# Attention value products in 64 by 64 tiles, with a newly planned order, in a fused attention and Hyena kernel on one core

## The chip, the cores and the metric

The kernel runs on one core of one Trainium2 chip. The metric is the device time in microseconds (us) of one execution; the median of three executions of the kernel before is 388.55 us (387.85 to 391.75). Smaller is better. All figures below come from these runs or from one execution that the hardware profiler recorded.

## The reference

Eight batches, twelve heads, 448 positions, head width 64. Attention with a softmax whose denominator has one more term, then a gated long convolution along the positions, with one projection in front and one behind:

```python
scores = scale * np.matmul(q, k.transpose(0, 1, 3, 2))      # (8, 12, 448, 448)
m = np.max(scores, axis=-1, keepdims=True)
e = np.exp(scores - m)
attn = e / (np.sum(e, axis=-1, keepdims=True) + np.exp(-m) + 1e-09)
x = np.matmul(attn, v)                                      # heads side by side: (8, 448, 768)
proj = x @ w_proj                                           # (8, 448, 2304)
x1, x2, x3 = ...                                            # three parts of 768 columns
x2_conv = irfft(rfft(x2) * rfft(filter_fft))                # along the 448 positions
out = (x1 * x2_conv * x3) @ w_out                           # (8, 448, 768) float32
```

Multiplied through by exp(m), the denominator is the plain sum of exp(scores) plus 1; this is how the kernel computes it, without a maximum.

## The kernel before

**Heads and groups.** The twelve heads of a batch form six pairs (`hp`, or `i` counted over all batches, 48 in all) and three groups of four heads (`Q`, 24 in all), each group two pairs (`u` = 0, 1). The 448 positions are split as 7 residues `j` of 64 positions each, because position p is row p // 7 and residue p % 7 of the tile as it is loaded (`load_rows`). Two heads of a pair sit in the lower and the upper 64 partitions (`w` = 0, 1).

**One group.** q, k and v of the group are loaded (L359) and cast to bf16 (L365, L370). q and k are transposed into `kqT`: on TensorE for the first two batches (L410, copied back at L415), by a transposing DMA afterwards (L426). Then come seven score units (`scores`, L597): in each, four matmuls of 64 by 64 weights and 448 moving columns stand abreast in the four quadrants of the array and write a pair of PSUM banks, and ScalarE takes the exponential of the pair into one of eleven `e` tiles (`exps`, L601). When all seven are there, each pair's value product follows (`values`, L616): 4 blocks of 128 positions, 7 residues and 2 heads make 56 matmuls. Each has 64 by 128 weights (a slice of `e`) and 65 moving columns (64 of v and one of ones, which gives the sum), and the two heads run abreast in the two row halves. The fourth block has only 64 positions, and its other 64 weight columns are zeros or the next head's: `e` is 64 columns longer than needed (`pads`, L1082). The result of a pair lies in a pair of banks, (128 positions, head, block, 65).

**Division and transposition.** VectorE adds one to the sums (L672), takes the reciprocal (L673) and multiplies (L674), pair by pair, into `xb`. `xb` is transposed into `xT`: in batch 0 on TensorE (L703, back at L712), in batches 1 to 7 by a DMA for three pairs at a time (L694).

**The dense part** of a batch (`dense`) folds `xT` on VectorE (L756, L761), projects it (`proj2`, L784), takes the spectrum (L811), multiplies (L825, L831), transforms back (`inverse`, L896), unfolds (L914 to L925), gates with the other two projections (`gate`, L857) and projects out (`project`, L969).

**The order.** No queue order is written down by hand. Every piece of work is a task with an engine, an estimated cost, a wanted time, tokens that it needs and makes, and PSUM banks that it takes and gives back; `Plan.run` is a list scheduler that goes through estimated time and fixes the order on each engine. Constants such as `ATT`, `SLOT`, `DENSE`, `PACE` and `LEAD` give the wanted times, `LOADS` and `LOAD` those of the weight loads. Eight PSUM banks are shared: a score unit and a value product take a pair (`sc`, `op`, two at most of each), all else one bank (`hy`). From the 22nd score unit on, scores come in runs of two units, and 42 of the 48 value products are "hosted": emitted in the same task right behind a run of scores (`score_runs`). While inputs are awaited at the start, `spin` (L1064 to L1073) and `fill` (L1055) issue idle matmuls. In `spin` some of them have 64 by 64 weights and 65 columns, some 64 by 128 weights and 65 columns.

The profile's names: PE is TensorE's matmul, PEld its weight load; each matmul of this kernel has a weight load of its own in front of it.

Of the kernel before, what the change touches and what calls it, by code (L numbers as in the profile page):

```python
# [256 lines left out]
def kernel(  # L257
# [15 lines left out]
    SPIN = 38  # L273
    EARLY0 = -7.81
    EARLY1 = -31.53
    NSINGLE, HOST = 22, 3
    ATT = [61.68, 19.06, 51.44, 90.48, 134.71, 184.75, 265.58, 265.83]
    SLOT = [7.18, 10.43, 5.20, 5.03, 0.93, 2.35, 4.65, 2.49]
    DENSE = [32.35, 109.75, 123.73, 146.53, 223.55, 274.11, 331.19, 326.09]
    PACE = [3.95, 1.73, 2.46, 3.56, 2.92, 2.20, 0.96, 1.78]  # L280
    FOLD = [-33.07, 7.97, -54.75, 19.23, -27.96, -50.67, -61.51, -23.76]
    BPS = -9.13
    WT = 12.35
    FT = -42.18
    LEAD = [25.24, 37.06, -25.73, 55.99, 16.70, 47.21, -33.20]
    VLATE = -3.09
    LOADS = ((1, 0), (1, 1), ("F", None), (0, None), (2, None), ("O", None))
    LOAD = [19.70, 3.41, 13.35, 32.51, 35.06, 49.84]
    XALL = (1, 2, 3, 4, 5, 6, 7)
    FOLD0 = [47.70, 1.87, 54.60]  # L290
# [6 lines left out]
    xbp = ctx.enter_context(tc.tile_pool(name="xbp", bufs=2))  # L297
# [26 lines left out]
    es = [const.tile([128, 2 * S + REM], BF16, name=f"e{i}") for i in range(NE)]  # L324
    rooms = [const.tile([128, 7 * 128], F32, name=f"room{i}") for i in range(NROOM)]
    kqn = [const.tile([128, 2, 7 * 128], BF16, name=f"kqn{i}") for i in range(NNAT)]
# [3 lines left out]
            "e": NE, "kqn": NNAT, "u": 1, "w": 1, "xf": 1,  # L330
# [43 lines left out]
    def arrive(b, g):  # L374
# [5 lines left out]
        for m, (name, x) in enumerate((("k", k), ("q", q), ("v", v))):  # L380
            n = 3 * Q + m
            to = rooms[n % NROOM]
            first = Q == 0 and name == "q"
            lead = LEAD[2 * m : 2 * m + 2] if not staged else (
                (EARLY0 if b == 0 else EARLY1) - 0.1 * m - (VLATE if m == 2 and b == 0 else 0),
                (-1.0 if b == 0 else 4.0) if m == 2 else 5.0,
            )
            add("ACT" if first else "SP", 0.6 if first else 0.52, -21.0 if Q == 0 and m < 2 else at - lead[0],
                lambda x=x, to=to, first=first: load_rows(nc.scalar if first else nc.sync, x, b, g, to),
                need=[("c" + "kqv"[(n - NROOM) % 3], (n - NROOM) // 3)] if n >= NROOM else [],  # L390
                make=[("s" + name, Q)], dma=1.35, run=1792)
            if name == "v":
                add("POOL", 0.96, at - lead[1], lambda to=to: cast_values(b, g, to), need=[("sv", Q)] + old,
                    make=[("cv", Q)])
                continue
            eng = "DVE" if Q == 0 else "POOL"

            def cast(m=m, to=to, eng=eng):
                cast_rows(nc.vector if eng == "DVE" else nc.gpsimd, kqn[Q % NNAT][:, m], to)

            add(eng, 0.56 if eng == "DVE" else 0.96, at - lead[1] + 0.01 * m, cast, need=[("s" + name, Q)], make=[("c" + name, Q)],
                take=[("kqn", Q)])
            if staged:
                hy = ("hy", ("T" + name, Q))

                def turn(m=m, hy=hy):
                    tb = bank2(hy)
                    for j in range(7):
                        c = slice(128 * j, 128 * j + 128)
                        nc.tensor.transpose(tb[:, c], kqn[Q % NNAT][:, m, c], ident_bf)  # L410

                on_act = False

                def turned(m=m, hy=hy, on_act=on_act):
                    (nc.scalar.copy if on_act else nc.vector.tensor_copy)(  # L415
                        kqT[b % 2][:, g, m].rearrange("p j c -> p (j c)"), bank2(hy)[:, 0 : 7 * 128]
                    )

                w = at - (3.5 if Q else 6.0)
                add("PE", 0.45, w, turn, need=[("c" + name, Q), "ident"], make=[("T" + name, Q)], take=[hy],  # L420
                    give=[("kqn", Q)])
                add("ACT" if on_act else "DVE", 0.83 if on_act else 0.55, w + 0.1, turned, need=[("T" + name, Q)],
                    make=[("kqT", Q)], give=[hy])
        if not staged:
            add("SP", 2.0, at - LEAD[6],
# [4 lines left out]
                need=[("ck", Q), ("cq", Q), ("S", Q - 2 * NQ, 6)], make=[("kqT", Q)], give=[("kqn", Q)], dma=1.7, late=0.5)  # L430
# [168 lines left out]
    def exps(n):  # L599
        EX[n] = e = es[n % NE]  # L600
        nc.scalar.activation(  # L601
            e[:, 0 : 2 * S].rearrange("p (u n j) -> p u n j", u=2, j=7),
# [4 lines left out]

    def values(i):
        Q, u = divmod(i, 2)
        b, g = divmod(Q, NQ)  # L610
        op = pair(("op", i))[:, :, 0 : NST * (DH + 1)].rearrange("p w (n d) -> p w n d", n=NST)
        for n in range(NST):
            for j in range(7):
                for w in range(2):
                    c = slice(64 * w, 64 * w + 64)
                    nc.tensor.matmul(  # L616
                        op[:, w, n, :],
                        EX[7 * Q + j][c, u * S + n * 128 : u * S + n * 128 + 128],
                        vn[b % 2][c, 2 * g + u, j, :],
                        start=(n == 0 and j == 0),  # L620
                        stop=(n == NST - 1 and j == 6),
                    )

    def value_args(i):
        Q, u = divmod(i, 2)
        return dict(
            need=[("e", Q), ("cv", Q), ("ones", Q // NQ % 2), "pads"] + ([("V", i - 1)] if u else []), make=[("V", i)],
            take=[("op", i)], give=[("e", 7 * Q + j) for j in range(7)],
        )

    def score_runs():
# [8 lines left out]
        for r, ns in enumerate(runs):  # L640
# [10 lines left out]
            add("PE", 0.2 + 0.155 * len(ns) + (1.0 if i is not None else 0.0), tau(2 * units[0][0], units[0][1] * 2 / 7), run,  # L651
# [6 lines left out]
        for i in range(2 * NQ * n_batches):  # L658
            if i not in hosted.values():
                a = value_args(i)  # L660
                add("PE", 1.1, tau(i // 2 * 2 + 2, 0.1 + 0.3 * (i % 2)), lambda i=i: values(i), need=a["need"], make=a["make"], take=a["take"],
                    give=a["give"])

    def attention(i):
        b, hp = divmod(i, NHP)

        def norm():
            op = pair(("op", i))[:, :, 0 : NST * (DH + 1)].rearrange("p w (n d) -> p w n d", n=NST)
            if ("xb", b) not in W:
                W["xb", b] = xbp.tile([128, NHP, NST, 128], BF16, name="xb")  # L670
            rec = small.tile([128, 2, NST], F32, name="rec")
            nc.vector.tensor_scalar_add(rec, op[:, :, :, DH], 1.0)  # L672
            nc.vector.reciprocal(rec, rec)  # L673
            nc.vector.tensor_tensor(  # L674
                W["xb", b][:, hp].rearrange("p n (w d) -> p w n d", w=2),
                op[:, :, :, 0:DH],
                rec[:].unsqueeze(3).to_broadcast([128, 2, NST, DH]),
                op=ALU.mult,
            )

        w = tau(i + 2, 0.5)
        add("DVE", 1.03, w - 0.5, norm,
            need=[("V", i)] + ([("X", NHP * (b - 1) - 1)] if b >= 2 else []),
            make=[("xb", i)], give=[("op", i)])
# [6 lines left out]
        def x_dma():  # L691
            x, xb = xT(), W["xb", b]
            gs = slice(hp - 2, hp + 1)
# [6 lines left out]
        def x_pe():  # L700
            tb = bank2(("hy", ("X", i)))
            for t in range(NST):
                nc.tensor.transpose(  # L703
                    tb[:, t * 128 : (t + 1) * 128], W["xb", b][:, hp, t, :], ident_bf
# [12 lines left out]
        if b in XALL:  # L717
            if hp % 3 == 2:
                ps = range(hp - 2, hp + 1)
# [8 lines left out]
    def dense(b):  # L728
# [213 lines left out]
        def I(dt):  # L942
# [3 lines left out]
            add("PE", 0.2, w, lambda: inverse(dt, hy), need=[("yh", b), "bt"], make=[("I", b, dt)], take=[hy],  # L946
# [89 lines left out]
    with (  # L1036
# [15 lines left out]

        def fill(i, count):
            for _ in range(count):
                nc.tensor.matmul(psum[:, 512 * i : 512 * i + 128], idle[:, 0:128], idle[:, 0:128])  # L1055
# [3 lines left out]
        def spin():  # L1059

            t = pair(("op", "spin"))
            half = (slice(0, 64), slice(64, 128))
            for _ in range(SPIN // 2):
                nc.tensor.matmul(t[:, 0, 0:128], idle, idle)  # L1064
            for _ in range(SPIN // 4):
                for u, r in enumerate(half):
                    for c in half:
                        nc.tensor.matmul(t[c, u, 0:65], idle[r, c], idle[r, 0:65])
            for _ in range(SPIN // 4):
                for u, r in enumerate(half):  # L1070
                    nc.tensor.matmul(t[:, u, 0:65], idle[r], idle[r, 0:65])
            for _ in range(SPIN // 4):
                nc.tensor.matmul(t[:, 0, 0:128], idle, idle)  # L1073

        add("PE", 4.0, -20.0, spin, need=["idle"], make=["spin"], take=[("op", "spin")], give=[("op", "spin")])
# [4 lines left out]
        def pads():  # L1080
            for e in es:
                nc.gpsimd.memset(e[:, 2 * S :], 0.0)  # L1082

        add("POOL", 1.5, 7.0, pads, make=["pads"], after=6.5)

        def ones(i):
            nc.gpsimd.memset(vn[i][:, :, :, DH : DH + 1], 1.0)
        for i in range(2):
            add("POOL", 0.7, (6.0, 24.0)[i], lambda i=i: ones(i), make=[("ones", i)],
# [52 lines left out]
```

## Time and profile before

| | |
|---|---|
| median of three executions | 388.55 us (387.85 to 391.75) |
| profiled execution: time / span | 387.59 us / 385.8 us |
| busy: PE, PEld | 370.8 us (96%), 228.2 us (59%) |
| busy: DVE, ACT, POOL | 257.8 us (67%), 258.9 us (67%), 75.9 us (20%) |
| instructions: PE matmuls, DVE, ACT | 5197, 658, 429 |
| DMA | 64.0 MB, mean 166 GB/s |
| mean granted TensorE clock | 0.991 |

The span runs from the first to the last instruction; 1.8 us of the time lie around it. A group of the profile is a line, an engine and an operation with its shapes: `64*128 64x65` are 64 by 128 weights, 64 rows of contraction and 65 moving columns. "xN | busy, mean | idle" are the count, the time in which at least one of the group was running, the mean duration of one, and the engine's idle time just before them with what ended it. Matmuls overlap in the pipeline, so 2688 value matmuls with a mean of 191 ns are busy for 51.5 us only. "issue" as releaser means that nothing the profile shows was waited for.

### The profile page before, as it was taken

The page shows a single profiled execution, that of the slowest core. Times are in us where ns is not written, and L with a number is a line of the kernel's source. Part 1 is how long each engine was busy: PE and PEld are TensorE (multiplying, and loading weights), DVE is VectorE, ACT ScalarE, POOL GpSimd, SP SyncE. Part 2 cuts the span into 40 slices and gives each one's busy share as a digit, 9 for nine tenths or more (in the row PEclk, how much of TensorE's full clock was granted, in tenths as well). Part 3 has the DMA queues.
Part 4 walks back from the last instruction along what each step waited for, and adds up shares of the span by engine and source line. Part 5 has one row for each costly group of instructions (what it writes and reads, how often), then busy time and mean ns, then how long its engine had stood idle before and what let it go on. Part 6 is the DMA issues. An engine that isn't in the chain of part 4 may idle for free.

```text
span 385.8 us, 12193 instructions
## 1 busy us (share of the span) xinstructions
PE 370.8 (96%) x5197; PEld 228.2 (59%) x5197; DVE 257.8 (67%) x658; ACT 258.9 (67%) x429; POOL 75.9 (20%) x100
## 2 busy tenths in 40 slices
PE   8969999979999999999999999999999999999996
PEld 6645675546645566556755566555755566657553
DVE  6677568884599539775689456784587355895760
ACT  4847858857687676767768667766768757644543
POOL 6746323132323321303201220010000000000000
PEclk9996999999999999999999999999999999999999
DMA  8999999999999998879556825412011302311024
GB/s 257 319 281 316 267 265 218 223 235 321 249 256 282 282 327 188 196 148 247 144 149 174 175 95 134 87 42 83 3 42 43 124 3 63 62 42 42 2 82 163
DMA packets 82998, 64.00 MB, mean 166 GB/s; under 512 B 56637, under 2 KB 79360, under 8 KB 82944
## 3 DMA queue, kind: packets, MB, share of 16 engines
q1 hardware_dynamic: 78192, 57.35, 57.3%
q0 software_dynamic: 4480, 5.41, 8.0%
q8 instruction: 40, 0.66, 0.7%
q10 hardware_dynamic: 272, 0.46, 0.3%
q14 instruction: 14, 0.11, 0.1%
HBM read 43.86 MB, written 11.01 MB: 142 GB/s over the span
## 4 chain that ended last, share of the span: by engine, by line
PE 79%; DVE 14%; ACT 2%; issue 2%; DMA 1%; DVEq 0%; ACTq 0%
PE psum L857 24%; PE psum L784 15%; PE psum L969 13%; PE psum L616 10%; PE psum L597 9%; PE psum L811 2%; PE psum L896 2%; ACT e L601 2%; DVE t L825 2%; DVE xb L674 2%; DVE cv L925 1%; PE psum L410 1%; DMA room<-in_k_dram 1%; DVE g L872 1%; DVE cw L916 1%
## 5 line engine op out<-in xcount | busy, mean ns | idle before, releaser
L601 ACT ACTIVATE e<-psum 128x896 bf16<-128x896 f32 x168 | 145.9, 922 | 33.6 <-PE psum L597 32.3
L857 PE MATMUL psum<-xT,wproj_bf 128*128 128x448 bf16 x576 | 121.7, 352 | 0.6 <-DVE xb L674 0.6
L857 PEld LDWEIGHTS <-wproj_bf 128*128 128x128 bf16 x576 | 53.0, 97 | 45.4 <-issue 3.9
L784 PE MATMUL psum<-wproj_bf,xf 128*113 128x384 bf16 x384 | 69.5, 328 | 0.0
L365 POOL CAST kqn<-room 128x896 bf16<-128x896 f32 x46 | 43.6, 950 | 105.3 <-DMA kqT<-kqn 51.4
L784 PEld LDWEIGHTS <-xf 128*113 128x113 bf16 x384 | 48.9, 132 | 14.4 <-issue 2.9
L616 PEld LDWEIGHTS <-e 64*128 64x128 bf16 x2688 | 45.4, 94 | 19.8 <-issue 18.5
L616 PE MATMUL psum<-vn,e 64*128 64x65 bf16 x2688 | 51.5, 191 | 3.1 <-issue 2.6
L969 PE MATMUL psum<-wout_bf,yT 128*128 128x384 bf16 x288 | 51.5, 326 | 2.5 <-DVE yT L940 2.5
L597 PE MATMUL psum<-kqT 64*64 64x448 bf16 x672 | 50.7, 368 | 1.3 <-DVE xb L674 0.9
L869 ACT CAST x<-psum 128x448 bf16<-128x448 f32 x48 | 25.7, 535 | 32.5 <-PE psum L857 31.5
L969 PEld LDWEIGHTS <-yT 128*128 128x128 bf16 x288 | 27.1, 98 | 23.3 <-DVE yT L940 3.7
L825 DVE TENSOR_TENSOR t<-xs,hrs 113x768 bf16<-113x768 bf16 (+1 forms) x64 | 35.6, 595 | 6.4 <-ACT xs L819 6.3
L981 ACT COPY osb<-psum 128x384 f32<-128x384 f32 x56 | 25.6, 490 | 19.7 <-PE psum L969 19.0
L796 DVE CAST x<-psum 113x384 bf16<-113x384 f32 x32 | 17.7, 554 | 30.9 <-PE psum L784 30.8
L370 POOL CAST vn<-room 128x896 bf16<-128x896 f32 x24 | 23.4, 974 | 72.3 <-PE psum L616 54.6
L872 DVE TENSOR_TENSOR g<-x,psum 128x448 bf16<-128x448 bf16 x48 | 29.6, 617 | 8.0 <-PE psum L857 7.2
L674 DVE TENSOR_TENSOR xb<-psum,rec 128x512 bf16<-128x512 f32 x48 | 33.2, 691 | 1.7
L672 DVE TENSOR_SCALAR rec<-psum 128x8 f32<-128x8 f32 x48 | 7.8, 162 | 38.2 <-PE psum L616 34.5
L819 ACT CAST xs<-psum 113x384 bf16<-113x384 f32 (+1 forms) x64 | 28.1, 500 | 4.0 <-PE psum L811 3.9
L905 ACT CAST cr<-psum 128x452 bf16<-128x452 f32 x48 | 24.8, 550 | 7.9 <-PE psum L896 6.2
L798 ACT CAST x<-psum 113x384 bf16<-113x384 f32 x32 | 15.4, 480 | 22.0 <-PE psum L784 21.8
(85 smaller groups left out, 296.9 us busy)
## 6 DMA issues: line engine op xcount, KB each, us to landing
room<-in_k_dram SPq DMA_DIRECT2D x24, 448.0 KB, 6.2
room<-in_v_dram SPq DMA_DIRECT2D x24, 448.0 KB, 5.9
room<-in_q_dram SPq DMA_DIRECT2D x23, 448.0 KB, 5.5
out_dram<-osb SPq DMA_DIRECT2D x24, 384.0 KB, 3.7
wproj_bf<-in_moe_w_proj_dram POOLq DMA_DIRECT2D x2, 1152.0 KB, 17.3
out_dram<-osb SPq DMA_DIRECT2D x8, 192.0 KB, 3.0
wproj_bf<-in_moe_w_proj_dram POOLq DMA_DIRECT2D x2, 576.0 KB, 12.9
wout_bf<-in_moe_w_out_dram POOLq DMA_DIRECT2D x1, 1152.0 KB, 17.2
```

Source lines behind the costliest of these rows:

```text
L365: eng.tensor_copy(to.rearrange("p (j u d) -> p u j d", u=2, j=7), src.rearrange("p (u j d) -> p u j d", u=2, j=7))
L597: nc.tensor.matmul(sc[c, u, 0:S], kqT[b % 2][r, g, 0, j, c], kqT[b % 2][r, g, 1, :, c])
L601: nc.scalar.activation(e[:, 0 : 2 * S].rearrange("p (u n j) -> p u n j", u=2, j=7), pair(("sc", ("S",) + divmod(n, 7)))[:, :, 0:S].rearran ...
L616: nc.tensor.matmul(op[:, w, n, :], EX[7 * Q + j][c, u * S + n * 128 : u * S + n * 128 + 128], vn[b % 2][c, 2 * g + u, j, :], start=(n == 0 ...
L674: nc.vector.tensor_tensor(W["xb", b][:, hp].rearrange("p n (w d) -> p w n d", w=2), op[:, :, :, 0:DH], rec[:].unsqueeze(3).to_broadcast([1 ...
L784: nc.tensor.matmul(pps[:FQ, :DCH], W["xf", b][:, pg, kt, 0:FQ], wproj_bf[:, kt, D + ch * DCH : D + (ch + 1) * DCH], start=(kt == 0), stop= ...
L819: nc.scalar.copy(L["xs", par, ch][:K, pg % 2, :], L["Z", pg, ch][:K, :DCH])
L825: nc.vector.tensor_tensor(t[:K], L["xs", par, ch][:K], h, op=ALU.mult)
L857: nc.tensor.matmul(p[:, :S], wproj_bf[:, kt, 2 * part * D + dt * 128 : 2 * part * D + (dt + 1) * 128], xT()[:, kt, 0:S], start=(kt == 0), ...
L869: nc.scalar.copy(L["x1", dt], p[:, :S])
L872: nc.vector.tensor_tensor(g[:, dt, :], L["x1", dt], p[:, :S], op=ALU.mult)
L969: nc.tensor.matmul(ops[:n, :DCH], y[:, dt, 0:n], wout_bf[:, dt, ch * DCH : (ch + 1) * DCH], start=(dt == 0), stop=(dt == NDT - 1),)
```

## The change

The value product of a pair is cut into blocks of 64 positions. Two such blocks are computed side by side in the two column halves of the array, so that four matmuls of 64 by 64 weights stand abreast instead of two of 64 by 128. The last 64 positions of both pairs of a group are put together as one block, so a group has 7 blocks: three in the first pair's task (84 matmuls), four in the second's (112). All results of a group lie in one pair of banks, which is taken by the first task and given back after one division for the whole group: two small operations over 2 by 7 sums and four multiplications. `e` loses its padding. The upper 64 partitions of the fourth block of `xb`, no longer written, are set to zero once; `xb` is two fixed tiles now. Transposing DMAs of `xT` cover four pairs and two pairs instead of three and three. `spin` and `fill` issue matmuls of up to 512 columns. All constants of the plan are new, and some costs in it are.

```diff
-    SPIN = 38
+    SPIN = 10
...
-    ATT = [61.68, 19.06, 51.44, 90.48, 134.71, 184.75, 265.58, 265.83]
+    ATT = [74.76, 12.23, 20.06, 84.10, 143.06, 182.87, 247.84, 302.15]
...
-    LOAD = [19.70, 3.41, 13.35, 32.51, 35.06, 49.84]
+    LOAD = [22.27, 25.04, -3.38, 24.31, 27.92, 66.85]
...
-    es = [const.tile([128, 2 * S + REM], BF16, name=f"e{i}") for i in range(NE)]
+    es = [const.tile([128, 2 * S], BF16, name=f"e{i}") for i in range(NE)]
+    xbs = [const.tile([128, NHP, NST, 128], BF16, name=f"xb{i}") for i in range(2)]
...
+    def outputs(Q):
+        return pair(("op", Q))[:, :, 0 : 7 * (DH + 1)].rearrange("p w (n d) -> p w n d", n=7)
+
     def values(i):
         Q, u = divmod(i, 2)
         b, g = divmod(Q, NQ)
-        op = pair(("op", i))[:, :, 0 : NST * (DH + 1)].rearrange("p w (n d) -> p w n d", n=NST)
-        for n in range(NST):
+        op = outputs(Q)
+        blocks = [(4 * u + n, [(u, 128 * n), (u, 128 * n + 64)]) for n in range(3)]
+        if u:
+            blocks.append((3, [(0, 384), (1, 384)]))
+        for n, part in blocks:
             for j in range(7):
                 for w in range(2):
-                    c = slice(64 * w, 64 * w + 64)
-                    nc.tensor.matmul(
-                        op[:, w, n, :],
-                        EX[7 * Q + j][c, u * S + n * 128 : u * S + n * 128 + 128],
-                        vn[b % 2][c, 2 * g + u, j, :],
-                        start=(n == 0 and j == 0),
-                        stop=(n == NST - 1 and j == 6),
-                    )
+                    r = slice(64 * w, 64 * w + 64)
+                    for h, (of, c) in enumerate(part):
+                        nc.tensor.matmul(
+                            op[64 * h : 64 * h + 64, w, n, :],
+                            EX[7 * Q + j][r, of * S + c : of * S + c + 64],
+                            vn[b % 2][r, 2 * g + of, j, :],
+                            start=(n == 0 and j == 0),
+                            stop=(n == 3 and j == 6),
+                        )
...
-            take=[("op", i)], give=[("e", 7 * Q + j) for j in range(7)],
+            take=[("op", Q)], give=[("e", 7 * Q + j) for j in range(7)],
...
-            add("PE", 0.2 + 0.155 * len(ns) + (1.0 if i is not None else 0.0), ...
+            add("PE", 0.29 + 0.155 * len(ns) + (0.8 if i is not None else 0.0), ...
...
         def norm():
-            rec = small.tile([128, 2, NST], F32, name="rec")
+            op = outputs(i // 2)
+            xb = xbs[b % 2]
+            rec = small.tile([128, 2, 7], F32, name="rec")
             nc.vector.tensor_scalar_add(rec, op[:, :, :, DH], 1.0)
             nc.vector.reciprocal(rec, rec)
-            nc.vector.tensor_tensor(... [128, 2, NST, DH] ...)
+            low, high = slice(0, 64), slice(64, 128)
+            for to, r, p, n in (
+                (xb[:, hp - 1, 0:3], slice(0, 128), slice(0, 128), slice(0, 3)),
+                (xb[:, hp, 0:3], slice(0, 128), slice(0, 128), slice(4, 7)),
+                (xb[:, hp - 1, 3:4], low, low, slice(3, 4)),
+                (xb[:, hp, 3:4], low, high, slice(3, 4)),
+            ):
+                nc.vector.tensor_tensor(
+                    to[r].rearrange("p n (w d) -> p w n d", w=2),
+                    op[p, :, n, 0:DH],
+                    rec[p, :, n].unsqueeze(3).to_broadcast([p.stop - p.start, 2, n.stop - n.start, DH]),
+                    op=ALU.mult,
+                )
-        add("DVE", 1.03, w - 0.5, norm, need=[("V", i)] + ..., make=[("xb", i)], give=[("op", i)])
+        if hp % 2:
+            add("DVE", 2.0, w - 0.5, norm, need=[("V", i)] + ...,
+                make=[("xb", i - 1), ("xb", i)], give=[("op", i // 2)])
...
-            if hp % 3 == 2:
-                ps = range(hp - 2, hp + 1)
+            turned = {3: (0, 4), 5: (4, 6)}.get(hp)
+            if turned:
+                ps = range(*turned)
...
+        wide = idle[:].unsqueeze(1).to_broadcast([128, 4, 128])
         def fill(i, count):
-            for _ in range(count):
-                nc.tensor.matmul(psum[:, 512 * i : 512 * i + 128], idle[:, 0:128], idle[:, 0:128])
+            for n in range(0, count, 4):
+                m = min(4, count - n)
+                nc.tensor.matmul(psum[:, 512 * i : 512 * i + 128 * m], idle, wide[:, 0:m])
...
-        def pads():
-            for e in es:
-                nc.gpsimd.memset(e[:, 2 * S :], 0.0)
...
         def ones(i):
             nc.gpsimd.memset(vn[i][:, :, :, DH : DH + 1], 1.0)
+            nc.gpsimd.memset(xbs[i][64:128, :, 3], 0.0)
```

## The prediction

> **What bounds the kernel now.** I read the busy table and the slices first, then the groups, then the order in time, and last the instruction starts in the trace.
>
> ```profile
> PE 370.8 (96%) x5197; PEld 228.2 (59%) x5197; DVE 257.8 (67%) x658; ACT 258.9 (67%) x429; POOL 75.9 (20%) x100
> PE   8969999979999999999999999999999999999996
> PEclk9996999999999999999999999999999999999999
> DMA  8999999999999998879556825412011302311024
> q8 instruction: 40, 0.66, 0.7%
> L616 PE MATMUL psum<-vn,e 64*128 64x65 bf16 x2688 | 51.5, 191 | 3.1 <-issue 2.6
> L674 DVE TENSOR_TENSOR xb<-psum,rec 128x512 bf16<-128x512 f32 x48 | 33.2, 691 | 1.7
> ```
>
> The reader sees an engine that sets the end: TensorE is busy 96%, the others two thirds or less. From the first projection (43.1 us) to its last matmul it waits for other engines some 8 us in all. So a microsecond taken out of TensorE's stream there is a microsecond gained, as long as nothing else holds TensorE up. The 2.6 us of "issue" in front of value matmuls is that something else. Here is one hosted product, then the stretch with that idle time (start us, us, what, xcount):
>
> ```profile
> 93.20 0.57 PE L597 MATMUL psum<-kqT 64*64 64x448 bf16 x8
> 93.71 1.07 PE L616 MATMUL psum<-vn,e 64*128 64x65 bf16 x56
> 94.70 0.70 PE L784 MATMUL psum<-wproj_bf,xf 128*113 128x384 bf16 x3
> ...
> 23.35 0.57 PE L597 MATMUL psum<-kqT 64*64 64x448 bf16 x8
> 23.86 0.90 PE L616 MATMUL psum<-vn,e 64*128 64x65 bf16 x45
> 27.35 0.35 PE L616 MATMUL psum<-vn,e 64*128 64x65 bf16 x11 [2.59 <-issue]
> 27.63 0.56 PE L410 MATMUL psum<-ident_bf,kqn 128*128 128x128 bf16 x7
> ```
>
> A product takes 0.99 us: 28 pairs abreast start 32 ns apart (0.88 us first to last), and the first matmul of another shape comes 120 ns after the last start. The second product stops after 45 of 56 matmuls, in the middle of a task that has no wait inside. The instruction queue explains it. It brought 0.66 MB in 40 packets for 10,394 TensorE instructions, so a packet is 256 instructions of 64 bytes. This stop stands before TensorE's instruction number 959; the one other stop without a releaser (20.88 us, 1.0 us) before number 703, 256 earlier. A packet began at 18.35 us and one at 25.00 us, took 1.0 us, and TensorE went on 1.5 and 1.4 us after their end. In all 39 packets that can be followed, no instruction of a block started sooner than 1.39 us after its packet had landed, and the packet began about when TensorE entered the block before. [...] Up to 130 us the packet begins 3.2 us after that entry (mean of 15; 1.6 to 5.0), later 0.1 us (mean of 24; up to 1.8). What differs is the load of the DMA engines (core's sum row: PE, PEld, DVE, ACT, POOL busy, clock, DMA share, GB/s):
>
> ```profile
> 43.00:130.00 87.00, 83.81 (x1219) 49.95 (x1217) 62.99 (x153) 62.97 (x105) 27.52 (x29) 1.00 1.11 254
> 130.00:386.00 256.00, 250.64 (x3266) 152.47 (x3263) 165.04 (x431) 168.25 (x291) 23.87 (x25) 1.00 0.45 115
> ```
>
> So a block must last 3.2 + 1.0 + 1.4 = 5.6 us early, and about 3.3 us later (0.9 us of start, an upper middle, because in a burst there is no time to look ahead), or TensorE stops. Before, no block after the first projection was short enough to stop it visibly; the shortest of all, by the rates here, has 3.5 us, in the start.
>
> **The change, part by part.** Counts of the changed kernel are from the order of its instructions as built.
>
> *Stream.* Value matmuls rise from 2688 to 4704, which is 1176 quads against 1344 pairs. A warm quad of this form isn't in the trace. The warm-up ran it at the half clock:
>
> ```profile
> L1068 PE MATMUL psum<-idle x36: 239/242/261, 3.2 to 3.6; 64*64 64x65 bf16 x36
> ```
>
> There quads start 55 ns apart, and pairs of 64 by 128 too (55 ns; 128 columns took 107 ns then, 56 ns later at the full clock). At the full clock pairs start 32 ns apart. I take 32 ns for the quad: at the half clock the two forms cost the same, and eight instructions are handed over in 12 ns in front of the scores. [...] After the first projection 2352 matmuls (37.6 us) become 4116 (32.9 us): -4.7 us; bounds -7.2 and +19.
>
> [...]
>
> *Changes of shape.* A 448-column matmul starts 189 ns before its successor of the same shape and 282 ns before one of another: 93 ns a change. Scores and values now have one shape: after the first projection 184 changes become 142, -3.9 us. With 0.4 us of small things TensorE's own work there falls from 329.7 to 320.7 us: **-9.0 us**.
>
> *Instruction supply.* The products take 9408 TensorE instructions instead of 5376, and 256 of them pass in 1.02 us instead of 2.05. Cut into blocks where the old ones lay, the changed order has early blocks of 3.1, 5.1, 2.6 and 1.4 us of work after the first projection (short by 2.5, 0.5, 3.0 and 4.2 against 5.6), one of 2.7 us near 130 us (2.9 or 0.6; I take 1.7), and later ones of 3.2, 2.6 and 1.0 (0.1, 0.7, 2.3). Sum **+15.0 us**. With the quickest early start seen (1.6 us) and 2.5 us later it is 6.7, with 0.9 us more for each block 21.
>
> *Start.* Six blocks instead of five lie ahead of the first projection (1698 instructions against 1436), three of them 1.2 to 1.7 us of work. Six times 5.6 us from 6.7 us on is 40 us: as late as now by supply alone. The waits for data there (some 7 us) come partly on top: +2 us, between -3 (only supply) and +8 (both add). The shorter warm-up lies in the wait for the first load and costs nothing; if it left the clock low, a few tenths.
>
> *Clock.* After the stop at 24.6 us the granted clock was half for 6.8 us (slice 4). Stops of 3 to 4 us may repeat that in dense stretches, 3.4 us a time: +2 us (0 to 7).
>
> *Cover.* While TensorE stands, the others catch up, which takes away part of its 8 us of waits: -4 us (0 to -8).
>
> *VectorE.* 48 times 162 + 203 + 691 ns become 24 times two small ones (14 columns, some 380 ns) and four multiplications. By the slope between L674 and the 448-column L872 (617 ns), 384 columns cost 543 and 128 cost 246: 1.96 us a group against 2.11, -3.6 us in all, hidden as VectorE is idle a third of the time. One block of 2 us instead of two of 1 us lets whatever stands behind it on VectorE, a copy that frees a bank above all, wait up to 1 us more; taken as 0 within the cover, bounds 0 and +8 (a rival below). *POOL, SP:* eleven memsets (1.5 us) go, two of 64 by 768 come (bounds 0.2 to 1.0 us each, from the memset of 64 columns and a cast of 896); POOL is 20% busy, its first value cast may come 0.6 us later, hidden by the start's wait. Transposing DMAs stay 14, with the same rows in all; the last two pairs' is smaller (3.2 us to land for three): 0, or half a microsecond gained once a batch where VectorE waits for it.
>
> **Sum**: -9.0 + 15.0 + 2 + 2 - 4 = +6.0 us on the profiled execution's 387.6 us, so 393.6; the median shown is 1.0 above that execution, and I say **394 us** (own range 389 to 404). A measurement of this kernel tells about 1% from no change: 384.7 to 392.4.
>
> **The rivals.**
> - *The supply keeps up, and it gets faster.* If packets start as promptly as later in the run (0.1 us, 2.5 us in all), two blocks fall short by 1.1 and 1.5 us and the start gains 1: 387.6 - 9.0 + 2.6 - 1 = 380, median 381. It decides as soon as a block needs under about 4 us. For: one packet begins 1.6 us after entry even early, and 134.5 us has 0.9 at a loaded DMA. Against: 13 of 15 early ones take over 2 us. 0.22.
> - *The stops fall where TensorE would wait anyway*: cover 8, start and clock 0: -2, median 386.6. For: the start is full of waits. Against: after 43 us the waits are small and elsewhere. 0.16.
> - *Quads at 55 ns*: 1029 quads after the first projection cost 23 us more, supply then 10: 412. For: the half-clock row is the only one of this form. [...] 0.04.
> - *Banks*: a pair of banks is held from the first product to the common division, 3.9 to 5.1 us between the products plus some 3, against 2.3 us twice. If dense work waits 0.4 us a group for a bank: +8, 402. For: eight banks for all. Against: VectorE and ACT have a third of their time left. 0.08.
>
> **How the numbers follow.** Forecast 0.50, of it 0.08 below 392.4. Faster: 0.22. Same: 0.16 + 0.08 = 0.24. Slower: 0.42 + 0.04 + 0.08 = 0.54. The range 381 to 405 goes from the first rival's time to beyond the bank rival's; below and above lie about 0.1 each.
>
> **What would show it.** Right: value quads 32 ns apart; no 93 ns between scores and values; idle "issue" of 1 to 5 us in the middle of value products, every one a multiple of 256 TensorE instructions from the others, most before 130 us; some 55 packets on the instruction queue; the granted clock low after them. Wrong: no such stops with TensorE's busy time near 360 us (first rival), quads far from 32 ns, or stops with VectorE or a bank as releaser.

## The result, and the profile after

The changed kernel takes 408.3 us in the median of four runs (407.5 to 410.9), the kernel before 388.2 us beside it: a ratio of 1.051, interval 1.044 to 1.058. It is slower by 5%. The forecast was 394 us with a range of 381 to 405: the direction and the mechanism hold, the size does not. The profiled execution took 407.5 us, with a span of 405.8 us.

From the page of the kernel after: busy times, TensorE's slices, the granted clock, the instruction queue, and the value products (count, busy and mean, idle before).

```profile
PE 369.9 (91%) x7085; PEld 228.5 (56%) x7085; DVE 255.3 (63%) x658; ACT 259.6 (64%) x429; POOL 76.3 (19%) x91
...
PE   8769697996599897999999999999999999989996
...
PEclk9887898999989999999999999999999999999999
...
q8 instruction: 55, 0.90, 1.0%
...
L623 PE MATMUL psum<-vn,e 64*64 64x65 bf16 x4704 | 51.1, 195 | 23.2 <-issue 22.8
```

TensorE is busy for the same 370 us, in a span that is 20 us longer. What is new is idle time in front of value matmuls that no releaser explains: 22.8 us of it, against 2.6 before. Some 18 us of it lie in the first third of the slices, where the granted clock has new dips too. The instruction queue brought 55 packets instead of 40. One such stretch in TensorE's order of time:

```profile
102.60 0.57 PE L596 MATMUL psum<-kqT 64*64 64x448 bf16 x8
103.28 0.88 PE L623 MATMUL psum<-vn,e 64*64 64x65 bf16 x84
103.98 0.87 PE L596 MATMUL psum<-kqT 64*64 64x448 bf16 x8
104.66 0.74 PE L623 MATMUL psum<-vn,e 64*64 64x65 bf16 x66
110.13 0.78 PE L623 MATMUL psum<-vn,e 64*64 64x65 bf16 x46 [4.74 <-issue]
110.85 3.83 PE L873 MATMUL psum<-xT,wproj_bf 128*128 128x448 bf16 x12
```

Two products of one group stand close together. The second runs dry after 66 of its 112 matmuls and stands for 4.7 us in the middle of a task. The 12 gate matmuls behind it take 3.8 us, where 12 took 2.4 us before: from 110.3 us on the granted clock is one half for 3.4 us.

### The profile page after: what moved, and what is told of

Its sections match the earlier page's. It is cut to its first block, busy times and chain, and to the rows that moved or that the text cites. A ratio compares the mean times of both kernels' runs of the same rounds, so it can differ in the third digit from the quotient of the medians.

```text
span 405.8 us, 15939 instructions
## 1 busy us (share of the span) xinstructions
PE 369.9 (91%) x7085; PEld 228.5 (56%) x7085; DVE 255.3 (63%) x658; ACT 259.6 (64%) x429; POOL 76.3 (19%) x91
## 4 chain that ended last, share of the span: by engine, by line
PE 80%; issue 8%; DVE 7%; ACT 3%; DMA 1%; DVEq 0%; ACTq 0%
PE psum L873 25%; PE psum L800 15%; PE psum L985 13%; PE psum L623 10%; PE psum L596 9%; PE psum L827 3%; ACT e L600 2%; PE psum L912 2%; PE psum L410 1%; DMA room<-in_k_dram 1%; DVE t L841 1%; DVE yh L847 1%; DVE cv L941 1%; DVE g L888 1%; PE psum L1074 1%
## 5 line engine op out<-in xcount | busy, mean ns | idle before, releaser
L600 ACT ACTIVATE e<-psum 128x896 bf16<-128x896 f32 x168 | 145.8, 921 | 48.7 <-PE psum L596 41.7
L873 PE MATMUL psum<-xT,wproj_bf 128*128 128x448 bf16 x576 | 124.1, 355 | 2.2 <-DVE g L888 1.6
L800 PE MATMUL psum<-wproj_bf,xf 128*113 128x384 bf16 x384 | 71.2, 331 | 3.2 <-issue 2.5
L623 PE MATMUL psum<-vn,e 64*64 64x65 bf16 x4704 | 51.1, 195 | 23.2 <-issue 22.8
L623 PEld LDWEIGHTS <-e 64*64 64x64 bf16 x4704 | 49.2, 107 | 31.8 <-issue 24.9
L596 PE MATMUL psum<-kqT 64*64 64x448 bf16 x672 | 51.8, 371 | 1.3 <-DVE xb L687 0.5
L985 PE MATMUL psum<-wout_bf,yT 128*128 128x384 bf16 x288 | 52.9, 326 | 0.0
L841 DVE TENSOR_TENSOR t<-xs,hrs 113x768 bf16<-113x768 bf16 (+1 forms) x64 | 33.0, 554 | 11.0 <-ACT xs L835 10.8
L687 DVE TENSOR_TENSOR xb<-psum,rec 128x384 bf16<-128x384 f32 (+1 forms) x96 | 36.1, 418 | 1.2
L678 DVE TENSOR_SCALAR rec<-psum 128x14 f32<-128x14 f32 x24 | 4.1, 171 | 46.9 <-PE psum L623 46.9
L596 PEld LDWEIGHTS <-kqT 64*64 64x64 bf16 x672 | 13.9, 106 | 29.1 <-issue 27.5
L814 ACT CAST x<-psum 113x384 bf16<-113x384 f32 x32 | 15.5, 483 | 22.8 <-PE psum L800 22.8
```

Of the source, the lines that this page charges most:

```text
L596: nc.tensor.matmul(sc[c, u, 0:S], kqT[b % 2][r, g, 0, j, c], kqT[b % 2][r, g, 1, :, c])
L600: nc.scalar.activation(e[:].rearrange("p (u n j) -> p u n j", u=2, j=7), pair(("sc", ("S",) + divmod(n, 7)))[:, :, 0:S].rearrange("p u (j ...
L623: nc.tensor.matmul(op[64 * h : 64 * h + 64, w, n, :], EX[7 * Q + j][r, of * S + c : of * S + c + 64], vn[b % 2][r, 2 * g + of, j, :], star ...
L687: nc.vector.tensor_tensor(to[r].rearrange("p n (w d) -> p w n d", w=2), op[p, :, n, 0:DH], rec[p, :, n].unsqueeze(3).to_broadcast([p.stop ...
L800: nc.tensor.matmul(pps[:FQ, :DCH], W["xf", b][:, pg, kt, 0:FQ], wproj_bf[:, kt, D + ch * DCH : D + (ch + 1) * DCH], start=(kt == 0), stop= ...
L841: nc.vector.tensor_tensor(t[:K], L["xs", par, ch][:K], h, op=ALU.mult)
```

## The experiments

All are set against the kernel before on the same chip. First the account of every profile that is used below, in us. "Own work" counts the matmuls behind the first projection at the rates of the prediction (a 448-column matmul 189 ns, a pair 32 ns, a change of shape 93 ns), with 33 ns for a quad (four matmuls abreast) as measured. "Stops" are the gaps from the start of one matmul to the start of the next at instruction numbers 703 plus or minus a multiple of 256, before and after the first projection; the idle time on the page, which begins at a matmul's modelled end, is 0.2 to 0.4 us less for each. "First projection" is the time at which the first projection starts. "Rest" is what is left behind the first projection, without half the time at the half clock and without the last 4.1 us, which belong to the last copy and store. It is a remainder, not a measurement: most of it is waits for other engines and for DMAs.

| kernel | span | first projection | own work | stops before / after it | half clock after it | rest |
|---|---|---|---|---|---|---|
| before | 385.8 | 43.1 | 329.5 | 3.8 / 0 | 0 | 9.1 |
| after | 405.8 | 50.5 | 321.6 | 11.0 / 17.3 | 6.8 | 8.8 |
| two abreast, new order | 390.9 | 38.6 | 324.7 | 2.1 / 2.1 | 10.2 | 16.2 |
| quads, old order | 421.3 | 58.2 | 327.0 | 15.2 / 20.0 | 10.2 | 7.0 |
| two abreast, quarters early | 386.9 | 40.9 | 325.0 | 0.6 / 0.4 | 3.4 | 14.8 |
| before with wide idle matmuls | 386.3 | 43.3 | 329.5 | 1.7 / 1.5 | 0.7 (at the very end) | 7.5 |

**Six of seven blocks two abreast, all else as in the changed kernel.** A group's 49 pair or quad times stay; the instructions fall to 10,138. The edit in `values`, with the seventh block first, right behind the scores:

```diff
-        blocks = [(4 * u + n, [(u, 128 * n), (u, 128 * n + 64)]) for n in range(3)]
-        if u:
-            blocks.append((3, [(0, 384), (1, 384)]))
+        blocks = [(3, [(0, 384), (1, 384)])] if u else []
+        blocks += [(4 * u + n, None) for n in range(3)]
...
+                    if part is None:
+                        c = u * S + (n - 4 * u) * 128
+                        nc.tensor.matmul(op[:, w, n, :], EX[7 * Q + j][r, c : c + 128], vn[b % 2][r, 2 * g + u, j, :], **flags)
+                        continue
```

> The changed kernel with its order, its common division and its one pair of banks a group, but the six full blocks of a group go back to 64 by 128 weights two abreast; only the seventh block, made of both pairs' last 64 positions, stays in 64 by 64 tiles, right behind the scores. TensorE's time for a group is the same (49 times 32 ns), its instructions fall from 14,170 to about 10,140. Theory (instruction supply): the stops at every 256th instruction, 27 us in all, go, and with them the half-clock stretches; about 40 changes of shape come back (3.9 us). The first projection starts at 43 us instead of 50, and the time is 380 to 387 us. Rival (the new order, the common division or the longer held banks cost the time): 400 us or more, whatever the form.

Measured: 389.5 us, ratio 1.0047 (1.0008 to 1.0086). Of the 20 us, all but some 2 are gone with the planned order, the common division, the banks and the planned start left as they were. So none of these makes the 20 us by itself. The stops fell from 28.3 to 4.2 us, and the first projection came at 38.6 us. The instruction queue's line is at the level of the kernel before again:

```profile
q8 instruction: 39, 0.64, 0.7%
```

The expected 380 to 387 was missed all the same. The profiled execution (392.6 us, the longest of the ten) shows one wait that the sum had not. TensorE in order of time:

```profile
45.99 1.30 PE L876 MATMUL psum<-xT,wproj_bf 128*128 128x448 bf16 x6
54.14 2.08 PE L803 MATMUL psum<-wproj_bf,xf 128*113 128x384 bf16 x6 [6.85 <-DMA wproj_bf<-in_moe_w_proj_dram]
```

The second quarter of the projection's weights, wanted at 25 us by the new plan behind a half load, lands late; the clock is at one half for 10.2 us from 49.6 us on. The changed kernel's profile, with its later start, has no wait for these weights. Whether this wait is what kept the time above 387 us is tried below.

**Quads in the old order.** The reverse: the kernel before, its division and its order, with each value matmul cut in two.

```diff
+                    for h in range(2):
                         nc.tensor.matmul(
-                            op[:, w, n, :],
-                            EX[7 * Q + j][c, u * S + n * 128 : u * S + n * 128 + 128],
+                            op[64 * h : 64 * h + 64, w, n, :],
+                            EX[7 * Q + j][c, u * S + n * 128 + 64 * h : u * S + n * 128 + 64 * h + 64],
```

> The kernel before with its order and its division pair by pair; only the value products are cut into 64 by 64 tiles, four abreast, the padded fourth block too: 112 matmuls a pair instead of 56, 28 quads instead of 28 pairs. Theory (instruction supply): TensorE's own time falls by some 4 us (no change of shape between scores and values), but its instructions rise from 10,394 to 15,770, and blocks of 256 run dry: stops of 25 to 45 us in all, time 405 to 425 us. Rival (the new order, the division or the banks): 384 to 389 us, as nothing of these is changed.

Measured: 426.0 us, ratio 1.098 (1.091 to 1.105). From its page:

```profile
q8 instruction: 61, 1.00, 1.0%
...
L617 PE MATMUL psum<-vn,e 64*64 64x65 bf16 x5376 | 58.3, 196 | 24.5 <-issue 24.2
```

TensorE's own work is 2.5 us less than before, the stops are 35.2 us against 3.8. The form alone, in a planned order that had run nearly without stops, brings them. The rival (order, division, banks) would have been 384 to 389.

**The supply by itself.** A kernel that does none of the computation and gives TensorE 1280 quads without a wait; the main part of its body, shortened:

```python
for n in range(48): nc.sync.dma_start(rooms[n % 5], ...)        # q and k, as the kernel loads them
for t in range(28): nc.sync.dma_start(flat[128 * t : ...], zero)
...                                                             # 16 wide idle matmuls
for n in range(1280):
    for w, r in enumerate(half):
        for c in half:
            nc.tensor.matmul(psum[c, 512 * w : 512 * w + 65], idle[r, c], idle[r, 0:65])
```

> Not the computation: 1280 quads of 64 by 64 weights and 65 columns without any wait, one after the other, while q and k are loaded and zeros are stored for the first 100 us or so; nothing else is done. Theory (instruction supply): TensorE goes through 256 instructions in about 1.05 us (33 ns a quad) and then stops; while the DMA engines are loaded a block comes every 5 to 6 us, and every 2.5 to 3.5 us after that; 1280 quads take 150 us or more. Rival (the stops in the kernel are waits for data that the records do not show): the stream runs through, 1280 times 33 ns = 42 us, with at most its first blocks late.

Measured: 184 us, in one execution. The waits, and two stretches (length, PE busy, PEld busy, DVE, POOL, clock, DMA share, GB/s), with the DMA loaded and without:

```profile
PE psum L48 <- issue: 96.7, 39, 5.1
```

```profile
40.00:88.00 48.00, 15.80 (x1024) 14.70 (x1024) 0.00 (x0) 0.00 (x0) 0.50 1.03 392
100.00:180.00 80.00, 43.03 (x2803) 40.02 (x2792) 0.00 (x0) 0.00 (x0) 0.50 0.02 5
```

39 waits without a releaser, every one 256 instructions behind the one before. The loaded 48 us pass 1024 matmuls, so 2048 instructions or 8 blocks, 6.0 us a block; the quiet 80 us 2803, so 21.9 blocks, 3.7 us a block. A block's matmuls take 1.8 us of this (the clock fell to one half at 12.3 us and stayed there, and a quad took 55 ns). In the trace the packet begins 2.5 to 3.9 us after TensorE enters the block before while the DMA is loaded, 1.0 to 1.7 us after when it is quiet; it takes 1.1 us, and TensorE goes on 1.2 to 1.6 us after its end. Data arrives for nobody here, so the rival (hidden waits for data, 42 us for the whole) is out.

The fetch of a block is seen to begin about when TensorE enters the block before: between 2.4 us ahead of that entry and 5.0 us after it in the kernel before, between 2.7 ahead and 4.3 after in the changed one, 1.0 to 3.9 us after it here. How many instructions TensorE holds was not measured.

**The old constants with the two-abreast form.**

```diff
-    ATT = [74.76, 12.23, 20.06, 84.10, 143.06, 182.87, 247.84, 302.15]
+    ATT = [61.68, 19.06, 51.44, 90.48, 134.71, 184.75, 265.58, 265.83]
...
-            add("PE", 0.29 + 0.155 * len(ns) + (0.8 if i is not None else 0.0), ...
+            add("PE", 0.2 + 0.155 * len(ns) + (0.95 if i is not None else 0.0), ...
```

> The kernel of the first experiment, with the plan's constants of the kernel before in place of the new ones (and the costs of a run of scores and a product near what the trace of before shows). Theory (instruction supply): no stops beyond those of before; 49 instead of 56 pair times of 32 ns a group save 5.4 us, and the time is 381 to 386 us. Against the first experiment it tells what the new order costs: if the order matters little, the two are within 4 us. Rival (common division and long held banks cost): above 390 us here too.

Measured: 393.2 us, ratio 1.014 (1.009 to 1.019). The expectation was missed, and the rival's time, above 390 us, is what came. The stops are 4.2 us in all, the own work is 5 us below that of the kernel before, and the rest is 16.1 instead of 9.1 us. The longest waits in it are 3.9 us for two transposing DMAs of `xT` and some 3 us for ScalarE's exponentials. How much of the rest comes from the common division and the banks that it holds longer, which the rival blamed, no run here separates; it can be a few us, not the 20. Against the first experiment the new constants are 4 us better for this form.

**Weight loads moved.** Seven kernels, to see what the late quarter costs. Two abreast, with the old wanted times of the weight loads:

```diff
-    LOAD = [22.27, 25.04, -3.38, 24.31, 27.92, 66.85]
+    LOAD = [19.70, 3.41, 13.35, 32.51, 35.06, 49.84]
```

> The first experiment's kernel (six blocks two abreast, the seventh in 64 by 64 tiles, the new order) with one constant list of the plan taken back: the wanted times of the weight loads, so that the first two quarters of the projection's weights are asked for at 3.4 and 19.7 us again instead of 22 and 25 us. Theory (in the first experiment TensorE stood 6.8 us at 47 us for weights that landed 21 to 27 us after issue): this wait goes, and the time is 380 to 385 us, faster than the kernel before by 0.5 to 2%. Rival (the new order is slower elsewhere too, or what is won there is lost behind it): 386 us or more.

With all constants of the start taken back (`EARLY0`, `EARLY1`, `BPS`, `WT`, `FT`, `VLATE`, `FOLD0`):

> As the kernel with the old weight loads, and all other constants that only place the start taken back as well (first input loads, tables, folding of the first batch). Theory: within 2 us of it, 380 to 386 us, since only the weight load was late. Rival: clearly faster than it (by 3 us or more), if other parts of the new start cost too.

The changed kernel itself with the old `LOAD`:

> The changed kernel with all products in 64 by 64 tiles and the wanted times of the weight loads taken back, nothing else. Theory (in the changed kernel the first projection is late by the stops of the instruction supply, and the weights land in their shadow): no gain beyond 3 us, 404 to 410 us, with stops at the same multiples of 256 instructions. Rival (the late weights are a cause of their own in the changed kernel): 398 to 403 us.

The first of the three with costs from the traces (0.2 and 0.95):

> The kernel with six blocks two abreast and the old weight loads, with the plan's costs of a run of scores and of a hosted product set to what the traces show (0.2 and 0.95 instead of 0.29 and 0.8), so that the order is planned from truer times. Theory (the order is worth a few us either way): 379 to 387 us, within 4 us of the same kernel with the new costs; a try for the fastest version.

Measured: 394.5 (ratio 1.013), 393.4 (1.014), 417.4 (1.075, interval 1.068 to 1.081) and 396.2 us (1.021). All four expectations were missed. (The second and the fourth did come within 2 and 4 us of the first, as expected, but at another level.) The wait for weights is gone in the three two-abreast ones, but each new order has others: the first of them stands 4.1 us at 123 us for a copy of ScalarE, and has the half clock behind it. In the changed kernel the old weight loads make things worse by 9 us, though the stops are fewer: 24.5 us against 28.3. What is more is the half clock behind the first projection, 13.7 us against 6.8, and the rest, 14.7 against 8.8. So moving the weights earlier wins nothing there; why this order is worse than the changed kernel's was not followed further than that account.

Then the smallest move, which keeps TensorE's order up to the first projection: the two quarter loads ahead of the half loads (`LOAD = [22.27, 25.04, -3.38, 31.00, 34.00, 66.85]`), the second quarter ahead of the first half (`[22.27, 22.90, -3.38, 26.50, 27.92, 66.85]`), and both quarters early (`[15.00, 18.00, -3.38, 26.00, 30.00, 66.85]`).

> The first experiment's kernel (six blocks two abreast, the seventh in 64 by 64 tiles, the new order) with the two quarter loads of the projection's weights ahead of the two half loads, which are wanted at 31 and 34 us; TensorE's order is the same up to the first projection and differs little behind it. Theory (late weights and the half clock behind the wait for them are what keeps the first experiment above the kernel before): the 6.8 us wait at 47 us and the 10 us of half clock go, 376 to 383 us, faster than before by 1 to 3%. Rival (as with the other weight loads: another order loses elsewhere what this wins): 386 us or more.

> As the previous one, with only the second quarter moved ahead of the first half load (wanted at 22.9 and 26.5 us). Theory: within 3 us of it, 377 to 385 us. Rival: a wait for the half that the gate needs takes the place of the wait for the quarter, 386 us or more.

> As the previous two, with both quarters wanted at 15 and 18 us, the halves at 26 and 30 us. Theory: no wait for weights at all; but inputs come later by the 1.2 MB in front of them (some 4 us at 300 GB/s), which delays the first projection from 38.6 to some 41 us: 378 to 386 us. Rival: above 388 us.

Measured: 391.3 us (1.0096, 1.0065 to 1.0127), 391.0 us (1.0088, 1.0050 to 1.0127) and 388.4 us (1.0011, 0.9965 to 1.0056). All three came out at their rivals' times. The wait for weights is 0.3 us in the first and 3.2 in the second, and neither is faster than the first experiment with its 6.8 us. So that wait does not explain why the two-abreast kernels miss 380 to 387. The last is level with the kernel before: 4.5 us less of own work, given back by 5.7 us more in the rest. All three stand 3.1 to 3.7 us at 123 to 128 us for the gate's product on VectorE; in the last (see the last section):

```profile
PE psum L876 <- DVE g L891: 3.1, 1, 3.1
```

No version tried here beats the kernel before.

**The kernel before with wide idle matmuls**, the one part of the change that lowers the number of instructions:

```diff
-    SPIN = 38
+    SPIN = 10
...
-            for _ in range(count):
-                nc.tensor.matmul(psum[:, 512 * i : 512 * i + 128], idle[:, 0:128], idle[:, 0:128])
+            for n in range(0, count, 4):
+                m = min(4, count - n)
+                nc.tensor.matmul(psum[:, 512 * i : 512 * i + 128 * m], idle, wide[:, 0:m])
...
+            for n in range(SPIN):
+                nc.tensor.matmul(t[:, n % 2], idle, wide)
```

> The kernel before, with one part of the change alone: the idle matmuls of the warm-up and of the fills have up to 512 columns instead of 64 to 128, with the same columns in all; TensorE's order is else the same, and its instructions fall from 10,394 to 10,144, nearly one block of 256, all of them ahead of the first projection. Theory (instruction supply holds the start too): the two stops of 1.0 and 2.8 us at 20 and 25 us shrink to 1 us or less together, the half-clock stretch behind them goes or shrinks, and the time falls by 2 to 5 us, to 382 to 385 us. Rival (the start is set by the arrival of the inputs, the stops lie in waits for them): within 1 us of the kernel before.

Measured: 388.0 us against 387.2, ratio 1.0014 (0.9985 to 1.0043): the rival's time. The start's stops went from 3.8 to 1.7 us and the sixth product began at 33.0 us instead of 37.3, but then TensorE stood 3.5 us for a division on VectorE, and the first projection came at 43.3 us.

```profile
PE psum L703 <- DVE xb L674: 3.5, 1, 3.5
```

So the shorter stops gained nothing here. The rival's reason, the arrival of the inputs, is not shown: the wait that took their place was for VectorE, whose step ahead of it took 2.6 us instead of 0.4 (last section).

## Why the prediction was wrong in size

By its own steps, profiled execution against profiled execution, +20.0 us against +6.0. The mechanism was right; three terms of the sum were too small, and one that was to pay for them paid nothing.

- *Stream and changes of shape*, -9.0: -7.9 by the rates as measured. At the full clock a quad takes 33 ns, not 32 (690 ns for the 20.75 quads between first and last start of a product). No run shows the rate of under 32 ns a quad that the bound of -7.2 us takes, nor 55 ns at the full clock; 55 ns came at the half clock alone, in the warm-up and in the kernel for the supply. The trace of before already spoke against 55: behind 43 us, at the start of a task, the second load of one tile starts 28 ns after the first for 64 by 64 weights, and 15 ns after it for 64 by 128 (medians). The first value matmul follows the last score quad after 179 ns instead of 282, so this step was there, 103 ns of it against the 93 assumed.
- *Instruction supply after the first projection*, +15.0: measured +17.3, block by block:

| stop at instruction | work in the block before | shortfall foretold | stop measured |
|---|---|---|---|
| 2239 | 3.1 us | 2.5 us | 2.9 us |
| 2751 | 5.1 | 0.5 | 0.4 |
| 3263 | 2.6 | 3.0 | 3.4 |
| 3775 | 1.4 | 4.2 | 4.9 |
| 5055 | 2.7 | 1.7 | 0.7 |
| 5567 | 3.6 (in the trace) | none | 2.7 |
| 8383 | 4.5 (in the trace) | none | 0.8 |
| 13503 | 1.0 | 2.3 | 1.6 |
| (two later blocks) | 3.2 and 2.6 | 0.1 and 0.7 | none |

 The early places come out of the instruction numbers alone. The two that were not foretold are packets that began 3.9 and 2.9 us after TensorE entered the block before, at 157 and 228 us, where 0.9 was assumed: the slow regime does not end at 130 us, it comes back with loaded DMA engines (DMA share 0.95 at 153 to 157 us, 1.14 at 222 to 225). So the first four stops were well foretold, 10.2 us against 11.6; that the later ones come near in sum, 4.8 us against 5.8, is luck, as 3.5 of the 5.8 stand where none was foretold.
- *Start*, +2: measured +7.4. **This is the first step that failed.** The bound of +8 held, the value chosen did not: I let the waits for data swallow most of the stops. The stops there rose from 3.8 to 11.0 us. One of them, and the first projection (its 50.54 is the 50.5 of the table):

```profile
40.20 0.54 PE L623 MATMUL psum<-vn,e 64*64 64x65 bf16 x40
44.08 0.77 PE L623 MATMUL psum<-vn,e 64*64 64x65 bf16 x72 [3.34 <-issue]
...
50.54 0.65 PE L800 MATMUL psum<-wproj_bf,xf 128*113 128x384 bf16 x3
```

 The first experiment, with the same planned start, is the better measure of what the stops did: its first projection came at 38.6 us, with 2.1 us of stops and no half clock ahead of it. The changed kernel has 8.9 us more of stops and 13.7 us of half clock there, and came 11.9 us later. If TensorE was busy throughout the half clock, that costs 8.9 + 6.8 = 15.7 us, of which the waits there swallowed some 4. So the new plan would have brought the start forward by some 4 us, and +7.4 is what was left of a larger loss.
- *Clock*, +2: 6.8 us at the half clock after the first projection, some 3.4 us if TensorE was busy throughout. Five dips, at 18, 28, 45, 66 and 110 us, each in or right behind a stop of 2.4 us or more; before, one. Two other stops of that length, at 95 and 159 us, have none.
- *Cover*, -4: **the second step that failed.** The rest is 8.8 us against 9.1, so nothing came of it. The other engines had time to catch up (ScalarE's exponentials sat idle 41.7 us for scores, against 32.3 before). That TensorE's remaining waits stood elsewhere in the order than its stops is the likely reason; no run tests it.
- *VectorE* at nothing: it fell from 257.8 to 255.3 us, and 48 large and 48 small multiplications took 36.1 us (418 ns a piece, 395 foretold). The banks' rival did not make the 20 us: the two-abreast kernel holds them as long and is within 0.5% of before. A smaller cost is open, as the two-abreast kernels spend 4.5 to 5 us less of own work and are no faster. The quarter loads of the weights moved to 22 us and beyond had no price in my sum; the first experiment shows a wait of 6.8 us for them, and the runs that took it away were not faster.
- *The range*: its upper end, 405, came from a rival's time. With the stream at -9, the upper bounds of the other terms (+21, +8, +7 and 0) lead from 387.6 to 415 us.

The rival in which the supply keeps up would have been 381 us; the measurement of the supply alone shows packets 2.5 us late or more for as long as the DMA is loaded, 14 in a row. One count in the text ahead of the prediction is off: 40 of the 48 products are hosted, not 42.

## What to carry to other kernels

Count instructions as well as columns: in these runs the fetch of a block of 256 TensorE instructions began from 2.7 us ahead of TensorE's entry into the block before to 5 us after it, and a new block took 3.7 us with idle DMA engines and 6 us with loaded ones, so a stream with a weight load and a matmul every 8 ns ran dry where no longer matmuls were mixed in. Packing four small tiles abreast bought 8 us of array time here and came with 28 us of stops, while four sevenths of the value products' instructions at nearly the same array time (two abreast, the odd block shared) came with 4. Look in a profile for idle time without a releaser in the middle of a task, and check whether the instruction numbers differ by a multiple of the block; and price a stop ahead of a data wait by what the wait still has left, not by what it had in another order.

## What the runs showed of the hardware beyond this

**VectorE beside GpSimd.** In the last experiment TensorE's 3.5 us wait was for VectorE. VectorE's lines come first, then GpSimd's at the same time:

```profile
31.93 0.40 DVE L756 TENSOR_TENSOR u<-xT 128x452 bf16<-128x452 bf16 x1
32.36 1.08 DVE L761 TENSOR_TENSOR xf<-u 128x226 bf16<-128x226 bf16 x2
33.36 2.60 DVE L756 TENSOR_TENSOR w<-xT 128x452 bf16<-128x452 bf16 x1
```

```profile
33.06 0.83 POOL L577 DMA_DIRECT2D wproj_bf<-in_moe_w_proj_dram  x1
33.89 1.81 POOL L365 CAST kqn<-room 128x896 bf16<-128x896 f32 x2
```

The same subtraction takes 0.39 us in the kernel before. Here it ends, after 2.60 us, 0.26 us after GpSimd's two casts have run. In the kernel with both quarters early an unfold step (L935) takes 1.11 us instead of a median of 0.39 while four casts follow one another; it and the four two-input steps around it take 3.0 us longer than their medians, just ahead of the 3.1 us wait. It is no rarity: in the kernel before, one such step (L916, at 125.68 us) takes 1.12 us against a median of 0.39 while two casts run (from 124.57 us, 1.98 us). The step of 2.60 us is recorded 0.5 us ahead of the casts. That the casts are the cause was not tested by an experiment of its own.

**The half clock without long stops.** In the kernels that compute, every stretch of half clock but the one at the end lasts 3.4, 6.8 or 10.2 us (6.83 us at 28.7 us in the kernel before; 6.83 us at 28.4 us and 3.41 us at 18.1, 45.4, 65.9 and 110.3 us in the changed one; 10.2 us from 49.6 us on in the first experiment), and one, at 18.1 us, came behind a stop of 2.4 us, with TensorE busy for 6.9 of the 7.5 us ahead of the stop. In the supply kernel the clock stayed at one half from 12.3 us to the end, through 80 us in which no stop was longer than 2.3 us, each behind 1.8 us of work.
